# A new written-out order for one core's local-global attention with gated projection, and a new order of its first loads

## The chip, the cores and the metric

One core of one Trainium2 chip runs the whole program. The metric is device time of one execution in microseconds. Each time comes from executions on the chip; the profile is one further execution, recorded by the hardware profiler.

## What is computed

Eight batches of eight heads, 512 local and 32 global tokens, head size 64. A local token attends to the 32 global tokens and to the local ones at most 32 positions away; a global token attends to all. The heads' outputs, side by side, are a 544 x 512 matrix x per batch. It goes through a causal depthwise convolution of five taps and a sigmoid (the gate), a value product, and an output product:

```python
s_g = scale * np.matmul(q_g, k_all.transpose(0, 1, 3, 2))
out_g = np.matmul(sm(s_g), v_all)
s_ll = np.where(mask, scale * np.matmul(q_l, k_l.transpose(0, 1, 3, 2)), -1e9)
a_l = sm(np.concatenate([s_lg, s_ll], axis=-1))
out_l = np.matmul(a_l, np.concatenate([v_g, v_l], axis=2))
...
for k in range(K):
    gate_pre += conv_w[k][None, None, :] * xp[:, k:k + S, :]
gate = 1.0 / (1.0 + np.exp(-gate_pre))
return (gate * (x @ w_val) @ w_out)
```

## The kernel before

**Units and batches.** The work is cut into 32 units (one batch and two heads each, four units to a batch) and, per batch, a global part. Each is a chain of named tasks. For unit u: `s` scores (TensorE, two PSUM banks), `mx` scaled and masked scores with their maximum (VectorE, two halves of four steps), `exp` (ScalarE, two halves of four), `t` transposes of the probabilities (TensorE, two halves), `tc` their copy out of PSUM, `av` weighted values (TensorE, two banks), `eps` and `norm` the division (VectorE), `xt` the second transposes (TensorE), `xc` their copy, `halo` the four columns of the tokens before, `xh`/`xl` the high and low parts of x for the split product, `tap` and `conv` the convolution (VectorE; for units 0 and 1 on TensorE as `pc`, with diagonal matrices `dg` made by GpSimd), `sig` the tanh. The global part of batch b has `gs gmax gexp gt gtc gav geps gnorm gx gxc`. Per batch, `g1.b.e.t` are the value products (three matmuls each, high and low parts), `gv gh gl` gate the result and split it, `g2.b.r.e` the output products, `ob.b.r` copies 128 rows out of PSUM and `st.b.r` stores them. All global rows of all batches go through one more such group, `g`, at the end. `w0` to `w7` are the eight weight slices, which arrive in 64 bits; eight VectorE steps each (`s0` to `s7`) and a copy `high` split them. `z` tasks are products of zeros, in which nothing is computed.

**Order.** Nothing is scheduled at run time. `ORDER` is one list of all tasks; each engine executes its own tasks in the order of that list, and waits only for what a task depends on. `name:ENGINE` says which engine does a task that several could do, `name@57` in which PSUM banks it lives (eight banks). `Plan.add` gives each task its engine and what it depends on, `Plan.order` walks the list.

**Buffers.** Rings limit how far ahead a task may run: two buffers `ob` (shared with the weight conversion), four each for q and k (one tile, 624 KB), v (975 KB), the probabilities and xc, ten for gate, xh and xl. A copy `ob` waits until the store of the copy two before it has landed.

**Loads.** The loads named in `FIRST` are issued on SyncE's queue ahead of all tasks, in that order (`q` is a unit's q and k, `v` its values, `w` a weight slice of 512 KB, `m` the mask and convolution weights, 148 KB). Each later load (`iq`, `iv`, `wi`) is a task on SyncE, held back to its place in the list by a dependence on the TensorE instruction emitted last before it:

```python
def transfer(out, in_):
    ins = nc.sync.dma_start(out, in_).ins
    if last_pe:
        tc.add_manual_dep(ins, last_pe[0].name, after, reason="a load's place in the line")
```

Stores are issued by ScalarE in its own order (`st`), whichever engine made the copy.

Of the kernel before, what the change touches and what calls it, by code (L numbers as in the profile page):

```python
# [57 lines left out]
xh1:ACT iq6 iq7 w3.s0:ACT av2@4 eps2:DVE norm2 w3.s1 w3.s2 w4.s0:ACT w3.s3 w3.s4 xl0:ACT w4.s1 t3.1@7 pc0.2 pc0.3
pc0.4 pco0:ACT xn1 xt2@1 xc2:ACT w3.s5 pc1.0@2 w4.s2 w3.s6 w4.s3 w3.s7 tc3.1:ACT av3@4 gav0.0@7 xl1:ACT eps3:ACT w4.s4
s4@60 norm3 w4.s5 gt0.1@3 xt3@5 w3.high:ACT xh2:ACT w5.s0:ACT w5.s1 w4.high:ACT w4.s6 mx4.0 w5.s2 gtc0.1 mx4.1 xn2  # L60
w4.s7 exp4.0 w5.s3 xc3:ACT tap3:ACT pc1.1 pc1.2 gav0.1 geps0:ACT s5@34 iv4 gnorm0 w2.s0:ACT xl2:ACT w2.s1 tap2:ACT
mx5.0 mx5.1 w5.high:POOL gx0@6 gxc0:ACT halo3:ACT exp4.1 xh3:POOL pc1.3 pc1.4 pco1:ACT t4.0@3 xn3 xl3:ACT exp5.0 iv5
gs1@60 iv7 w2.s2 w2.s3 w2.high:ACT iv6 halo2:DVE s6@24 t4.1@5 tc4.1:ACT tc4.0:ACT w5.s4 w5.s5 gmax1.0 gexp1.0 conv3.0
w2.s4 conv2.0 mx6.0 exp5.1 exp6.0 gmax1.1 gexp1.1 w2.s5 mx6.1 w2.s6 exp6.1 w5.s6 g1.0.0.0@6 g1.0.0.1 g1.0.0.2 fix0
g1.0.0.3 g1.0.1.0@0 g1.0.1.1 w2.s7 gt1.0@2 t5.0@7 tc5.0:ACT av4@4 eps4:ACT t6.0@1 g1.0.1.2 w5.s7 norm4 t5.1@7
tc6.0:ACT gtc1.0 fix1 conv3.1 sig0 gv.0.0 xt4@1 xc4:ACT xh4:POOL s7@54 mx7.0 tc5.1:ACT av5@2 tap4:ACT wi6 iq8 mx7.1
sig1 eps5:ACT exp7.0 gav1.0@7 gt1.1@5 gtc1.1 conv3.2 norm5 g1.0.1.3 gv.0.1 wi7 t6.1@4 gh.0.0:ACT tc6.1:ACT conv3.3 iq9
iq10 iq11 exp7.1 gh.0.1:ACT gav1.1 geps1:DVE av6@5 eps6:ACT xt5@2 conv2.1 xn4 g1.0.2.0@0 g1.0.2.1 w6.s0:ACT xc5:ACT
xh5:ACT sig3 gnorm1 gx1@3 gxc1:ACT norm6 xt6@4 xn5 xl5:ACT halo4:ACT w6.s1 conv2.2 iv8 w6.s2 conv2.3 sig2 w6.s3 w6.s4
w7.s0:ACT xc6:ACT halo6:ACT gl.0.1 xh6:ACT tap6:ACT w7.s1 iv9 w6.s5 gl.0.0 w7.s2 w6.high:POOL g1.0.2.2 g1.0.2.3 s8@75  # L70
t7.1@6 tc7.1:ACT t7.0@3 tc7.0:ACT mx8.0 exp8.0 g1.0.3.0@2 g1.0.3.1 xn6 xl6:ACT xl4:ACT g1.0.3.2 mx8.1 exp8.1 w6.s6
g1.0.3.3 gv.0.2 t8.0@3 gv.0.3 tc8.0:ACT av7@6 s9@05 w7.s3 gs2@13 gh.0.3:ACT gh.0.2:ACT eps7:DVE norm7 xt7@6 mx9.0
# [5 lines left out]
g2.0.2.3 g2.0.3.0@0 g2.0.3.1 gt2.0@5 g2.0.3.2 s11@31 tap8:ACT xh8:ACT mx11.0 iq15 gtc2.0 gav2.0@2 gt2.1@5 ob.0.2:ACT
gtc2.1 st.0.1 t10.0@4 tc10.0:ACT t10.1@7 tc10.1:ACT av9@5 eps9:ACT mx11.1 exp11.0 norm9 gav2.1 geps2:ACT gnorm2 av10@3
eps10:ACT conv5.3 t11.0@7 exp11.1 tc11.0:ACT xt9@1 gx2@2 gxc2:DVE xc9:ACT tap9:ACT g2.0.3.3 ob.0.3:ACT s12@52 sig6  # L80
halo8:DVE iv13 norm10 xh9:ACT gs3@63 t11.1@1 tc11.1:ACT conv8.0 mx12.0 exp12.0 halo9:ACT xt10@5 xc10:ACT halo10:ACT
xh10:ACT g1.1.0.0@0 mx12.1 iv12 xl9 gmax3.0 gmax3.1 sig7 s13@21 gexp3.0 conv8.1 mx13.0 conv9.0 conv9.1 sig4 gexp3.1
# [5 lines left out]
gav3.0@4 gt3.1@2 gtc3.1 xl11 t13.1@7 xt12@0 tc13.1:ACT gl.1.1 gv.1.3 av13@1 eps13:DVE xc12:ACT tap12:ACT gav3.1 gl.1.2
geps3:DVE gnorm3 s15@73 gh.1.3:ACT gl.1.3 gx3@0 gxc3:ACT exp14.0 mx15.0 exp15.0 mx15.1 halo12:ACT xh12:ACT iv17 iq18
iq19 exp15.1 mx14.1 conv12.0 norm13 conv12.1 conv12.2 conv11.2 conv12.3 conv11.3 g2.1.0.0@4 g2.1.0.1 g2.1.0.2 g2.1.0.3  # L90
t14.0@7 g2.1.1.0@3 xl10 ob.1.0:ACT tc14.0:ACT g2.1.1.1 g2.1.1.2 s16@42 t15.1@5 xt13@0 exp14.1 t14.1@1 t15.0@6 xc13:ACT
tc14.1:ACT g2.1.1.3 g2.1.2.0@7 tc15.0:ACT av14@0 tc15.1:ACT av15@5 mx16.0 mx16.1 tap13:ACT exp16.1 t16.1@4 xh13:DVE
exp16.0 eps14:DVE norm14 xt14@2 st.1.0 tc16.1:ACT xc14:ACT halo14:ACT iv16 g2.1.2.1 tap14:ACT eps15:DVE xh14:ACT
ob.1.1:DVE st.1.1 norm15 xl13 s17@30 mx17.0 mx17.1 iv18 gs4@41 gmax4.0 exp17.0 halo13:ACT conv13.0 t16.0@6 gexp4.0
xt15@3 xc15:ACT tap15:ACT g2.1.2.2 g2.1.2.3 ob.1.2:ACT st.1.2 xh15:ACT exp17.1 t17.0@0 tc17.0:ACT gt4.0@4 iv19 gtc4.0
sig12 tc16.0:ACT conv13.1 gmax4.1 gexp4.1 halo15:DVE conv15.0 conv13.2 conv13.3 conv15.1 xl15 xl12 conv14.0 conv14.1
iq20 conv14.2 xl14 conv14.3 sig14 conv15.2 conv15.3 sig13 iq21 g2.1.3.0@3 g2.1.3.1 g2.1.3.2 g2.1.3.3 g1.2.0.0@1
ob.1.3:ACT st.1.3 g1.2.0.1 g1.2.0.2 g1.2.0.3 gv.2.0 gh.2.0:DVE g1.2.1.0@5 g1.2.1.1 g1.2.1.2 g1.2.1.3 av16@6 gav4.0@2
gv.2.1 s18@04 s19@31 mx18.0 t17.1@5 g1.2.2.0@0 eps16:ACT exp18.0 norm16 xt16@6 g1.2.2.1 mx18.1 gh.2.1:DVE gl.2.1
tc17.1:ACT exp18.1 sig15 gt4.1@4 gtc4.1 mx19.0 g1.2.2.2 t18.0@7 exp19.0 gav4.1 geps4:ACT av17@4 tc18.0:ACT mx19.1  # L100
xc16:DVE xh16:ACT gnorm4 gx4@3 gxc4:ACT halo16:ACT tap16:DVE t18.1@1 g1.2.2.3 g1.2.3.0@3 tc18.1:ACT gl.2.0 iq22
g1.2.3.1 conv16.0 conv16.1 conv16.2 iq23 conv16.3 sig11 g1.2.3.2 g1.2.3.3 iv22 exp19.1 s20@67 sig16 eps17:DVE av18@1
gv.2.2 gv.2.3 norm17 gh.2.2:DVE gh.2.3:DVE xt17@0 xc17:ACT gl.2.2 halo17:ACT mx20.0 exp20.0 gl.2.3 xl16 eps18:DVE
norm18 mx20.1 tap17:DVE conv17.0 conv17.1 conv17.2 xh17:ACT xl17 g2.2.0.0@3 g2.2.0.1 g2.2.0.2 t19.1@6 tc19.1:ACT iv21
iv20 g2.2.0.3 g2.2.1.0@4 g2.2.1.1 xt18@0 xc18:ACT conv17.3 tap18:ACT g2.2.1.2 g2.2.1.3 ob.2.1:ACT sig17 g2.2.2.0@2
exp20.1 g2.2.2.1 gs5@46 gmax5.0 gmax5.1 st.2.1 s21@01 xh18:DVE t19.0@4 xl18 tc19.0:ACT t20.0@5 tc20.0:ACT t20.1@6
mx21.0 g2.2.2.2 mx21.1 g2.2.2.3 ob.2.2:DVE tc20.1:ACT av19@4 eps19:DVE av20@0 norm19 eps20:DVE gexp5.0 gt5.0@6
# [870 lines left out]
```

## Time and profile before

| | us |
|---|---|
| median of 3 runs | 363.06 (360.9 to 363.09) |
| the profiled execution | 362.68 |
| its span, first to last instruction | 360.9 |
| TensorE busy | 349.5 |
| VectorE busy | 307.2 |
| ScalarE busy | 233.6 |
| GpSimd busy | 10.4 |

The time of an execution is its span and 1.8 us around it. Matmuls overlap in the pipeline and their ends are modelled, so a busy TensorE may still be losing time; the profile's view by stretches gives busy time and the granted clock for any part of the span. A wait is put down to what came last. SPq and ACTq are the queues on which SyncE and ScalarE issue DMAs.

### The profile page before, as it was taken

What the parts mean: (1) busy time and instruction counts of PE and PEld (TensorE: products, weight loads), DVE (VectorE), ACT (ScalarE), POOL (GpSimd) and SP (SyncE); (2) the same over time, 40 slices, a digit from 0 to 9 for tenths busy, and PEclk for the clock granted to TensorE, in tenths of its full rate; (3) what the DMA queues carried; (4) which work ended last, traced back from release to release, by engine and by line L of the source; (5) the groups of instructions that cost most, each with busy time, mean ns of one, the idle gap of its engine ahead of it and who ended that gap; (6) DMA issues with size and microseconds to landing.
All of it is one profiled execution on the core that took longest, in us unless ns stands there. A gap on an engine that the chain in (4) does not pass through costs nothing.

```text
span 360.9 us, 14693 instructions
## 1 busy us (share of the span) xinstructions
PE 349.5 (97%) x6339; PEld 282.1 (78%) x6339; DVE 307.2 (85%) x1027; ACT 233.6 (65%) x587; POOL 10.4 (3%) x23
## 2 busy tenths in 40 slices
...
GB/s 298 396 399 293 177 272 256 370 127 344 121 348 281 113 177 319 248 14 308 189 181 307 139 322 146 107 143 181 289 96 3 4 39 81 0 58 35 83 59 58
DMA packets 17104, 66.59 MB, mean 185 GB/s; under 512 B 1808, under 2 KB 3984, under 8 KB 17040
## 3 DMA queue, kind: packets, MB, share of 16 engines
...
## 4 chain that ended last, share of the span: by engine, by line
PE 82%; DMA 7%; DVE 6%; ACT 2%; issue 1%; SPq 1%; DVEq 0%; ACTq 0%
PE psum L646 26%; PE psum L674 20%; PE psum L522 8%; PE psum L533 8%; PE psum L497 7%; DMA out_dram<-ob 4%; PE psum L552 4%; DMA v<-in_vw_dram 3%; PE psum L462 2%; PE psum L618 2%; PE psum L442 2%; PE psum L423 1%; DVE gate L234 1%; DVE pm L234 1%; PE psum L444 1%
## 5 line engine op out<-in xcount | busy, mean ns | idle before, releaser
L234 DVE SCALAR_TENSOR_TENSOR gate<-xc,cw,gate 128x512 f32<-128x512 f32 x120 | 87.6, 749 | 4.8 <-ACT xc L329 2.6
L516 ACT ACTIVATE pm<-pm,mx 128x128 f32<-128x128 f32 x256 | 80.8, 393 | 11.8 <-DVE mx L234 11.2
L234 DVE CUSTOM_DVE_ANT_0 pm<-psum,small 128x128 f32<-128x128 f32 x256 | 57.3, 287 | 4.7 <-PE psum L497 4.7
L646 PE MATMUL psum<-xh,wvh 128*128 128x512 f32 x128 | 53.0, 414 | 0.0
L674 PE MATMUL psum<-woh,gh 128*128 128x512 f32 x128 | 52.3, 408 | 0.0
L646 PE MATMUL psum<-xl,wvh 128*128 128x512 f32 x128 | 50.9, 397 | 0.0
L646 PE MATMUL psum<-xh,wvl 128*128 128x512 f32 x128 | 50.5, 394 | 0.0
L674 PE MATMUL psum<-woh,gl 128*128 128x512 f32 x128 | 50.2, 392 | 0.0
L674 PE MATMUL psum<-wol,gh 128*128 128x512 f32 x128 | 50.0, 390 | 0.0
L522 PE MATMUL psum<-ident,pm 128*128 128x128 f32 x256 | 39.2, 281 | 3.5 <-ACT ob L322 3.1
L522 PEld LDWEIGHTS psum<-ident,pm 128*128 128x128 f32 x256 | 29.5, 142 | 12.0 <-ACT ob L322 4.0
L322 ACT ACTIVATE ob<-psum 128x512 f32<-128x512 f32 x26 | 15.4, 592 | 36.3 <-PE psum L674 23.2
L497 PE MATMUL psum<-qk 64*32 64x128 f32 x2048 | 36.8, 276 | 0.9 <-issue 0.9
L329 ACT COPY pts<-psum 128x512 f32<-128x512 f32 x54 | 30.5, 583 | 9.8 <-PE psum L522 9.4
L497 PEld LDWEIGHTS psum<-qk 64*32 64x32 f32 x2048 | 29.4, 107 | 8.7 <-issue 5.2
L533 PE MATMUL psum<-v,pts 128*32 128x65 f32 x2048 | 35.0, 221 | 1.2 <-DMA v<-in_vw_dram 0.7
L533 PEld LDWEIGHTS psum<-v,pts 128*32 128x32 f32 x2048 | 30.5, 109 | 7.1 <-issue 4.6
L234 DVE SCALAR_TENSOR_TENSOR gv<-gate,psum 128x512 f32<-128x512 f32 x32 | 21.5, 683 | 10.8 <-PE psum L646 10.7
L630 ACT ACTIVATE gate<-gate 128x512 f32<-128x512 f32 x32 | 20.0, 629 | 13.5 <-DVE gate L234 12.9
L646 PEld LDWEIGHTS psum<-xh,wvl 128*128 128x128 f32 x128 | 24.3, 190 | 5.6
L646 PEld LDWEIGHTS psum<-xh,wvh 128*128 128x128 f32 x128 | 24.5, 192 | 4.9 <-DVE gm L234 0.4
L674 PEld LDWEIGHTS psum<-woh,gl 128*128 128x128 f32 x128 | 24.0, 188 | 5.3
...
## 6 DMA issues: line engine op xcount, KB each, us to landing
...
wraw<-in_w_val_dram SPq DMA_DIRECT2D x4, 512.0 KB, 12.5
...
```

Of the source, the lines that this page charges most:

```text
L234: ins = made(*args, **kwargs)
L322: A.activation(out=out, in_=in_, func=AF.Copy, scale=by)
L329: A.copy(out, in_)
L442: on_pe(T.transpose(pt[:96, 1 + a, :], pg[:, 96 * a:96 * a + 96], ident))
L497: on_pe(T.matmul((sx, sy)[h][32 * j:32 * j + 32, i, :], qkt[rows, 32 * m:32 * m + 32], qkt[rows, k0:k0 + P], start=True, stop=True))
L516: A.activation(out=pm[:, h, i, :], in_=pm[:, h, i, :], func=AF.Exp, bias=mx[:, c:c + 1], scale=-1.0)
L522: on_pe(T.transpose(pt[:, i, :], pm[:, h, i, :], ident))
L533: on_pe(T.matmul(ax[32 * j:32 * j + 32, h, E1 * i:E1 * i + E1], pts[:, h, i, 32 * j:32 * j + 32], vt[:, block_win(4 * i + j), h, :], start ...
L552: on_pe(T.matmul(xt[:, P * i:P * i + P], xs[:, i].rearrange("p h d -> p (h d)"), ident, start=(i == 0 or u not in XP), stop=(u not in XP), ...
L630: A.activation(out=g, in_=g, func=AF.Tanh, scale=0.5)
L646: on_pe(T.matmul(box["pv", e], w[:, e, t * P:t * P + P], x, start=(t == 0 and q == 0), stop=(t == NDT - 1 and q == 2)))
L674: on_pe(T.matmul(box["po", r], g[:, e, rs], w[:, e, :], start=(e == 0 and q == 0), stop=(e == NDT - 1 and q == 2)))
```

## The change

`ORDER` is replaced by another list of the same 1,480 tasks besides the `z` tasks: another sequence on every engine, other PSUM banks, other engines for some steps (about equally many go from ScalarE to VectorE and back; a few more go to GpSimd), and other places for the later loads and stores. The zero products are six in three tasks (`z1.0`, `z4.1`, `z1.2`) instead of three in two. In `FIRST`, q and k of unit 2 and the values of unit 0 go ahead of the first weight slice, and the values of units 2 and 3 go ahead of the third and fourth. No task's code changes. The two lists have over a hundred lines each; the beginning, two later places and the end are shown.

```diff
 ORDER = """
-s0@50 s1@12 cw dg0 mx0.0 exp0.0 t0.0@5 mx0.1 mx1.0 w0.s0:ACT exp1.0 z2.0@3 t1.0@7 tc0.0:ACT s2@34 wi4 w0.s1 w0.s2
-exp0.1 t0.1@6 w0.s3 w0.s4 w0.high:ACT mx2.0 mx2.1 tc0.1:ACT z1.1@0 av0@0 dg1 eps0:DVE gs0@35 mx1.1 exp2.1 norm0 exp2.0
-xt0@2 gmax0.0 exp1.1 t1.1@0 gexp0.0 iq4 s3@41 tc1.0:ACT xc0:ACT gmax0.1 gexp0.1 tc1.1:ACT w1.s0:DVE w1.s1 w1.s2 wi5
...
-w7.s4 w7.s5 av8@1 gl.0.3 t9.0@7 tc9.0:ACT g2.0.0.2 w7.s6 gexp2.0 iq12 tap7:ACT iv10 w7.s7 s10@53 mx10.0 exp10.0 iv11
...
-av11@6 mx13.1 iq16 iq17 xl8 eps11:ACT norm11 iv14 exp13.0 tap10:ACT conv10.0 conv9.2 conv10.1 t12.0@5 tc12.0:ACT
...
-g2.4.0.0@2 s28@16 gv.4.3 mx28.0 tc26.1:ACT av26@4 gav6.1 iv30 tc27.0:ACT av27@0 eps26:ACT norm26 geps6:DVE xt26@4
-exp28.0 gnorm6 gx6@7 mx28.1 g2.4.0.1 g2.4.0.2 gh.4.3:ACT iv31 gl.4.3 g2.4.0.3 g2.4.1.0@6 g2.4.1.1 g2.4.1.2 eps27:DVE
...
-xl26 iv29 ob.4.0:ACT st.4.0 halo26:ACT conv24.2 conv24.3 tap26:ACT xh25:ACT xl25 g2.4.1.3 g2.4.2.0@5 g2.4.2.1 g2.4.2.2
-ob.4.1:ACT conv26.0 conv26.1 conv26.2 sig24 xc27:ACT xh27:ACT conv25.2 conv25.3 conv26.3 tap27:ACT st.4.1 halo27:DVE
-conv27.0 conv27.1 g2.4.2.3 ob.4.2:ACT st.4.2 sig26 iv28 conv27.2 conv27.3 g2.4.3.0@2 t28.1@1 tc28.1:ACT g2.4.3.1
-g2.4.3.2 g2.4.3.3 ob.4.3:ACT st.4.3 g1.5.0.0@3 g1.5.0.1 gs7@64 gmax7.0 s29@01 mx29.0 gmax7.1 exp29.0 mx29.1 exp29.1
-t28.0@2 tc28.0:DVE g1.5.0.2 g1.5.0.3 gv.5.0 g1.5.1.0@6 gexp7.0 g1.5.1.1 g1.5.1.2 g1.5.1.3 gv.5.1 t29.1@0 tc29.1:DVE
...
+cw s0@31 dg0 dg1 s1@62 mx0.0 exp0.0 mx0.1 mx1.0 exp0.1 s2@10 wi4 mx2.0 mx2.1 exp1.0 z1.0@4 t1.0@7 tc1.0:DVE mx1.1
+exp2.0 exp2.1 t0.0@5 tc0.0:DVE exp1.1 w0.s0:DVE w0.s1 t0.1@4 tc0.1:ACT z4.1@3 av0@6 eps0:ACT gs0@40 t2.1@3 tc2.1:ACT
+w0.s2 w0.s3 norm0 xt0@2 iq4 iq5 gmax0.0 t1.1@6 w0.s4 w0.s5 xc0:ACT t2.0@3 halo0 s3@74 wi5 tc1.1:ACT z1.2@5 av1@5 w0.s6
+gmax0.1 iq6 xh0:ACT mx3.0 mx3.1 w1.s0:ACT gexp0.1 pc0.0@0 iq7 w1.s1 xn0 tc2.0:ACT eps1:DVE norm1 w0.s7 w1.s2 w1.s3
+xt1@3 exp3.0 w1.high:POOL exp3.1 t3.0@4 xc1:DVE xl0:ACT pc0.1 w1.s4 gexp0.0 w0.high:ACT w1.s5 w1.s6 w1.s7 tc3.0:ACT
...
+w6.s7 iq12 g2.0.0.0@2 tap4:ACT iv9 iq13 g2.0.0.1 w7.s6 gl.0.2 xn7 xl7:ACT s10@67 w7.s7 gh.0.3:ACT gl.0.3 gexp2.0
...
+mx13.0 xl9 g1.1.0.1 mx13.1 exp13.1 g1.1.0.2 g1.1.0.3 norm11 xt11@5 xc11:ACT halo10:ACT conv8.0 conv8.1 conv8.2 t12.0@2
...
+g2.4.0.2 iv29 tap22:ACT conv22.0 g2.4.0.3 conv23.1 ob.4.0:ACT st.4.0 g2.4.1.0@3 exp28.1 g2.4.1.1 g2.4.1.2 g2.4.1.3
+g2.4.2.0@1 g2.4.2.1 g2.4.2.2 g2.4.2.3 ob.4.1:DVE st.4.1 conv23.2 halo25:ACT conv22.1 eps27:ACT exp28.0 iq31 ob.4.2:ACT
+conv22.2 xt26@2 iv31 g2.4.3.0@0 g2.4.3.1 g2.4.3.2 g2.4.3.3 g1.5.0.0@3 conv22.3 g1.5.0.1 norm27 xt27@5 ob.4.3:DVE
+conv23.3 xc26:ACT iv28 xl23 g1.5.0.2 g1.5.0.3 conv24.3 t28.0@7 gv.5.0 g1.5.1.0@1 xc27:DVE tc28.0:DVE sig21 s29@03
+gs7@46 mx29.0 exp29.0 gmax7.0 t28.1@2 tap26:DVE iv30 mx29.1 tc28.1:DVE g1.5.1.1 t29.0@4 g1.5.1.2 g1.5.1.3 exp29.1
...
+xh25:ACT halo26:DVE xl25 t30.1@5 tc30.1:ACT g2.5.0.0@6 g2.5.0.1 g2.5.0.2 gav7.1 conv25.0 gh.5.3:DVE st.4.3 tc30.0:ACT
+av30@3 tc31.0:DVE av31@1 xt29@0 tap27:DVE gl.5.3 g2.5.0.3 st.4.2 conv25.1 conv25.2 g2.5.1.0@5 g2.5.1.1 g2.5.1.2
...
+conv30.3 gh.7.0:ACT gl.7.0 ob.6.1:DVE ob.5.2:ACT st.5.2 sig30 sig29 gv.7.1 gv.7.2 g1.7.3.3 g2.7.0.0@4 gh.7.1:DVE
+gl.7.1 gh.7.2:DVE gl.7.2 st.6.1 ob.6.3:ACT gv.7.3 gh.7.3:DVE gl.7.3 ob.5.0:DVE g2.7.0.1 gxl1 g2.7.0.2 st.6.3 g2.7.0.3
+g2.7.1.0@0 st.5.0 ob.7.0:ACT st.7.0 gconv3 sigg3 g2.7.1.1 g2.7.1.2 g2.7.1.3 g2.7.2.0@3 gxh3:DVE gxl3 gtap1:DVE gconv1
+ob.7.1:ACT st.7.1 gtap2:DVE g2.7.2.1 g2.7.2.2 g2.7.2.3 g2.7.3.0@0 g2.7.3.1 g2.7.3.2 gxh0:DVE gxl0 g2.7.3.3 g1.g.0.0@2
+ob.7.3:ACT gconv2 g1.g.0.1 gxl2 g1.g.0.2 g1.g.0.3 sigg2 gtap0:DVE gconv0 sigg0 gv.g.0 st.7.3 gh.g.0:DVE gl.g.0
...
 """
...
-FIRST = "q0 m0 q1 w0 q2 v0 q3 w1 v1 w2 v2 w3 v3"
+FIRST = "q0 m0 q1 q2 v0 w0 q3 w1 v1 v2 w2 v3 w3"
```

## Rows read from the trace of the kernel before

**Rows 1.** The page, its first part: busy time of each engine, its share of the span, and its instructions.

```profile
PE 349.5 (97%) x6339; PEld 282.1 (78%) x6339; DVE 307.2 (85%) x1027; ACT 233.6 (65%) x587; POOL 10.4 (3%) x23
```

**Rows 2.** The chain of waits in order of time, pieces in which TensorE runs one kind of step without a gap: start, us, engine, line, instructions. L646 are the value products, L674 the output products, L497 a unit's scores (64 instructions), L533 its weighted values (64), L522 its transposes (8), L423 a batch's global scores (32), L462 one half of the global values (40), L618 one tap of a convolution on TensorE (2).

```profile
20.39 0.86 PE psum L618 x2
...
42.11 1.08 PE psum L423 x32
...
57.81 0.71 PE psum L462 x40
...
272.26 0.87 PE psum L522 x8
273.13 1.95 PE psum L533 x128
...
277.60 1.96 PE psum L497 x128
...
301.49 10.99 PE psum L646 x48
312.92 10.91 PE psum L674 x48
...
345.69 5.65 PE psum L646 x48
351.34 5.46 PE psum L674 x24
```

**Rows 3.** TensorE's timeline: the second transposes (of the normalized values xs) of units 2, 16, 27, 28 and of the last one (30). Start us, us, engine, line, operation, tiles, shape, count.

```profile
30.34 0.60 PE L552 MATMUL psum<-ident,xs 128*128 128x128 f32 x4
...
154.15 0.63 PE L552 MATMUL psum<-ident,xs 128*128 128x128 f32 x4
...
252.20 0.60 PE L552 MATMUL psum<-ident,xs 128*128 128x128 f32 x4
...
275.60 0.60 PE L552 MATMUL psum<-ident,xs 128*128 128x128 f32 x4
...
312.32 0.60 PE L552 MATMUL psum<-ident,xs 128*128 128x128 f32 x4
```

**Rows 4.** The table by stretches of the span: busy time of each engine with its instructions in brackets (TensorE, its weight loads, VectorE, ScalarE, GpSimd), then the granted clock as a share of 2.4 GHz, the mean busy share of the DMA engines, and GB/s.

```profile
0.00:27.00 27.00, 22.97 (x533) 14.64 (x533) 19.96 (x101) 19.69 (x51) 8.00 (x19) 1.00 0.96 364
27.00:120.00 93.00, 92.84 (x2109) 73.34 (x2105) 90.43 (x322) 83.14 (x211) 2.40 (x4) 1.00 0.66 252
120.00:252.00 132.00, 131.92 (x2711) 109.22 (x2700) 121.80 (x425) 90.43 (x236) 0.00 (x0) 1.00 0.54 195
...
262.80:265.90 3.10, 0.04 (x4) 0.00 (x1) 3.06 (x17) 0.60 (x1) 0.00 (x0) 0.99 0.19 68
265.90:269.20 3.30, 3.30 (x10) 2.82 (x11) 1.39 (x9) 2.94 (x9) 0.00 (x0) 0.50 0.22 82
269.20:357.00 87.80, 87.59 (x864) 73.67 (x863) 59.70 (x142) 30.54 (x71) 0.00 (x0) 1.00 0.11 40
```

**Rows 5.** The timeline of the first 30 us, all engines, in order of time; in brackets how long the engine stood before the row, and for what. The rows are the scores of unit 1 (weight loads), the first two maxima of unit 0, its first group of exponentials, the scores of unit 2, the issue of v3 on SyncE's queue, three groups of exponentials in one, and the weighted values of unit 0.

```profile
6.72 0.89 PEld L497 LDWEIGHTS psum<-qk 64*32 64x32 f32 x64 [0.15 <-DMA qk<-in_qk_dram]
...
6.96 0.29 DVE L234 CUSTOM_DVE_ANT_0 pm<-psum,small 128x128 f32<-128x128 f32 x1 [0.46 <-PE psum L497]
...
7.18 0.28 DVE L234 CUSTOM_DVE_ANT_0 pm<-psum,small 128x128 f32<-128x128 f32 x1
...
7.30 1.28 ACT L516 ACTIVATE pm<-pm,mx 128x128 f32<-128x128 f32 x4 [5.09 <-DVE mx L234]
...
10.63 1.16 PE L497 MATMUL psum<-qk 64*32 64x128 f32 x64
...
12.19 3.51 SPq L347 DMA_DIRECT2D v<-in_vw_dram  x1
...
13.02 3.62 ACT L516 ACTIVATE pm<-pm,mx 128x128 f32<-128x128 f32 x12
...
13.29 1.11 PE L533 MATMUL psum<-v,pts 128*32 128x65 f32 x64 [0.69 <-DMA v<-in_vw_dram]
```

**Rows 6.** The place near 84 and the place near 265: a piece of the chain of waits (a store that was waited for); two v loads on SyncE's queue (start, time of the two issues); ScalarE's timeline with the issue of st.4.1 and the copy ob.4.3; TensorE's with t28.0; and the time from issue to landing of the DMAs that read the copies ob, from the view of that tile.

```profile
83.85 6.45 DMA out_dram<-ob
...
252.83 3.78 SPq L347 DMA_DIRECT2D v<-in_vw_dram  x2
...
256.55 0.34 ACTq L855 DMA_DIRECT2D out_dram<-ob  x1
...
265.25 0.60 ACT L322 ACTIVATE ob<-psum 128x512 f32<-128x512 f32 x1 [3.79 <-DMA out_dram<-ob]
...
265.90 1.11 PE L522 MATMUL psum<-ident,pm 128*128 128x128 f32 x4 [3.06 <-ACT ob L322]
...
DMA to landing us min/median/max: 2.0/2.6/8.3
```

**Rows 7.** The timelines of VectorE and TensorE at two hand-overs: gl.0.3 (VectorE) and the first output product that reads it, the second step of unit 11's normalization (xs) and its transposes.

```profile
76.88 0.69 DVE L234 TENSOR_TENSOR gl<-gv,gh 128x512 fp32r<-128x512 f32 x1
...
78.92 0.39 PE L674 MATMUL psum<-woh,gh 128*128 128x512 f32 x1
...
106.01 0.69 DVE L234 TENSOR_TENSOR xs<-psum,mx 128x512 f32<-128x512 f32 x1
...
107.56 0.60 PE L552 MATMUL psum<-ident,xs 128*128 128x128 f32 x4
```

More of the change, by code (lines that the diff above doesn't have):

```diff
@@ L58 @@
[L58 to L72, printed above, removed]
@@ L78 @@
[L78 to L82, printed above, removed]
@@ L88 @@
[L88 to L107, printed above, removed]
@@ L123 @@
-g1.4.1.0@0 g1.4.1.1 g1.4.1.2 g1.4.1.3 halo23:ACT conv23.0 eps24:DVE norm24 conv23.1 conv23.2 exp26.0 t26.0@2
-tc26.0:DVE gv.4.0 gv.4.1 gh.4.1:DVE conv23.3 exp27.1 xt24@1 xc24:ACT xh24:DVE gav6.0@3 sig23 av25@4 eps25:DVE norm25
-gh.4.0:ACT tap24:ACT xl24 iq30 iq31 gl.4.0 gl.4.1 exp26.1 xl23 gt6.1@1 g1.4.2.0@6 g1.4.2.1 g1.4.2.2 g1.4.2.3 xt25@7
-t27.1@0 tc27.1:DVE g1.4.3.0@5 gtc6.1 gv.4.2 gh.4.2:DVE xc25:ACT gl.4.2 g1.4.3.1 g1.4.3.2 t26.1@4 t27.0@0 g1.4.3.3
-g2.4.0.0@2 s28@16 gv.4.3 mx28.0 tc26.1:ACT av26@4 gav6.1 iv30 tc27.0:ACT av27@0 eps26:ACT norm26 geps6:DVE xt26@4
@@ new lines @@
+exp2.0 exp2.1 t0.0@5 tc0.0:DVE exp1.1 w0.s0:DVE w0.s1 t0.1@4 tc0.1:ACT z4.1@3 av0@6 eps0:ACT gs0@40 t2.1@3 tc2.1:ACT
+w0.s2 w0.s3 norm0 xt0@2 iq4 iq5 gmax0.0 t1.1@6 w0.s4 w0.s5 xc0:ACT t2.0@3 halo0 s3@74 wi5 tc1.1:ACT z1.2@5 av1@5 w0.s6
+gmax0.1 iq6 xh0:ACT mx3.0 mx3.1 w1.s0:ACT gexp0.1 pc0.0@0 iq7 w1.s1 xn0 tc2.0:ACT eps1:DVE norm1 w0.s7 w1.s2 w1.s3
+xt1@3 exp3.0 w1.high:POOL exp3.1 t3.0@4 xc1:DVE xl0:ACT pc0.1 w1.s4 gexp0.0 w0.high:ACT w1.s5 w1.s6 w1.s7 tc3.0:ACT
+av2@5 eps2:DVE norm2 gt0.0@1 xh1:ACT xn1 halo1 w4.s0:DVE xl1:ACT w4.s1 w4.s2 w4.s3 gtc0.0 w4.s4 pc0.2 pc0.3 pc0.4
```

134 lines of the change are left out of this document (85 added, 49 removed).

## Prediction, before the changed kernel was run

> **What bounds the kernel now.** The page's table of engines comes first: TensorE is busy for 97% of the span, VectorE 85%, ScalarE 65% [rows 1]. That share is an average, and TensorE's ends are modelled, so the second view is the chain of waits, read for runs of one kind with nothing between them. They give what each step costs when TensorE streams [rows 2]: 48 value products in 10.99 us, 48 output products in 10.91, the last (global) group 5.65 and 5.46, a unit's scores 0.98 (1.96 for two), its weighted values 0.975, its eight transposes of probabilities 0.87, a global score step 1.08, a global value step 0.71, one tap of a convolution on TensorE 0.86. A batch's products are 21.9 us, eight batches 175.2, the global group 11.1; 32 units of scores, values and transposes are 31.4 + 31.2 + 27.8; their second transposes, at half of 0.87, 13.9; 16 global value steps 11.4, 8 global scores 8.6, 80 global transposes at 0.109 are 8.7, ten taps 8.6, small ones (10 products of 512 columns and 8 single transposes, at 0.229 and 0.109) 2.7. Together 331 us. The change keeps all of them, so only about 30 us of the 360.9 can move.
>
> Where these 30 us lie is read from TensorE's own timeline: start of a second transpose, less the work ahead of it in the order. I call this the lag. It is 12.7 us at unit 2 (30.34, with 17.6 us of work ahead), 17.8 at unit 16 (154.15, 136.4), 20.65 at unit 27 (252.20, 231.55), 25.7 at unit 28 (275.60, 249.9) and 26.0 at the last (312.32, 286.3) [rows 3]; from the end of the last product, 356.8, to the end of the span another 4.1 pass [rows 2]. So 12.7 go in the first 30 us, 8 drip away over the next 220 (changes of kind, stalls of tenths), 5 go in one place near 265, and the last 90 us lose nothing. The table by stretches says who else is near its limit: VectorE is busy 90.4 of 93 us between 27 and 120 and 121.8 of 132 up to 252, but 59.7 of 87.8 at the end [rows 4]. For two thirds of the kernel VectorE is a second bound right behind TensorE.
>
> **Part 1: the first loads.** The 13 loads are the same; unit 2's q and k and v0 pass the first weights. Before, s1 starts at 6.72, as its data lands, and s2 at 10.63 [rows 5]. A 624 KB load at the 364 GB/s of the stretch 0 to 27 takes 1.7 us [rows 4], so q2 now lands near 8.4. But s2 also writes a bank that the eighth maximum of unit 0 sets free; the maxima start at 6.96 and follow one another 0.22 us apart [rows 5], so s2 goes at about 8.8, 1.8 us earlier. This is lost again at the next step. The new order puts six groups of exponentials on ScalarE ahead of tc0.1, which av0 needs: 7.30 plus six times 1.2 (12 in 3.62) is 14.5, plus 0.6 for the copy 15.1 [rows 5]. Before, av0 waited for v0 until 13.29. So v0's earlier landing buys nothing, and av0 is 1.8 us later. The conversion of w0 starts near 13.7 instead of 8.5; nothing of TensorE asks for w0 before g1.0.0.0, 25 us later, and the VectorE time freed is taken by maxima and by two copies. Following both orders on with these durations, the set up to av2 (scores 0 to 3, seven transposes, av0 to av2, gs0, xt0, xt1, two taps, xn0, gt0.0: 14.35 us, the same set in both) ends at 27.1 before and near 26.7 after. SyncE's later queue does not move: its ring is full until 15.7 either way (12.19 + 3.51, rows 5), and 8.6 MB come first in both. I take -0.3 us, bounds -1.0 and +1.0. Six filler products instead of three run while TensorE has nothing else: 0, at most 0.7 if all three sit on the path.
>
> **Part 2: VectorE in the first 120 us.** The counts per step stay; who does them changes (net +6.6 us for VectorE, most of it late, by counting both lists at row durations). What matters is the work of VectorE ahead of a step that TensorE waits for, against TensorE's own ahead of the consumer. For unit 11's normalization it was 103.1 against 91.1, and is 101.7 against 87.9: 1.8 us less margin. The margin before was 0.9 (its norm done at 106.7, its transposes at 107.56). For gl.0.3 there is 2.9 less, with 1.4 before (done 77.6, used 78.92) [rows 7]. So TensorE would wait some 1.5 us at the first and 0.9 at the second. These do not add: the second is the same queue, already late. What remains is the excess over the lag that before reaches anyway (17.8 at unit 16 against some 18.2), 0.4 to 0.9. I take +0.6; bounds 0 and +1.8.
>
> **Part 3: the stall near 265.** Here ScalarE stands before ob.4.3 for the buffer of ob.4.1, whose store went out at 256.55 and landed 8.3 us later; the median is 2.6 [rows 6]. Ahead of it lie four v loads of 975 KB, the last two issued at 252.83. The copy starts at 265.25, frees bank 2, and t28.0 starts at 265.90. TensorE stood 3.06 us, and in the stretch behind it the granted clock is 0.50, that is 1.2 GHz, for 3.3 us, in which four transposes and six products ran that cost 1.8 at 2.4 GHz [rows 2, 4, 6]. The lag says 5.0 for the whole place; less 0.3 for ordinary drip it is 4.7. In the new order the four v loads of this batch stand apart (iv29 before g2.4.0.3, iv31 after g2.4.2.3, iv28 after ob.4.3, iv30 after gs7), so at most one load and iq31 lie near st.4.1; t28.0 no longer uses the bank of g2.4.3; and ob.4.3 is on VectorE. I take -4.7, bounds -5.0 and 0.
>
> The row shows a store that landed only once the loads ahead of it were through. The Trainium skill, page "DMA: Bandwidth & Descriptors", section "Queues, rings and completion order", says that each DMA engine takes turns between the queues, packet by packet. By that rule the store on ScalarE's queue would go on at about half its rate beside the loads, which adds an estimated 0.7 us (256 KB at 364 GB/s) to 2.6; the loads would not be the cause, and setting them apart would give nothing. The trace's 8.3 us speaks against it, and so does the 6.45 of a second store, at 83.85, with loads about it [rows 6]; but these are two stores.
>
> **Part 4: the late half.** VectorE has 80 us of steps left from g1.5.0.0 on, where it had 61, against 92 of TensorE. Three places are close: xl23 behind ob.4.3 (0.45 us before g1.5.0.3), gl.7.3 (0.4 before g2.7.0.3), gxl2 behind three global convolutions (0.7 before g1.g.0.2), each worked out by following the lists from the last step at which VectorE waits for TensorE. ob.4.3 on VectorE is a new wait: behind it stand conv23.3, xl23, conv24.3 and gv.5.0, and g1.5.0.3 waits for xl23. With a landing of 2.6 us it costs nothing; with one of 6 it costs 2 to 3. The stores st.4.2 and st.4.3 now wait 24 to 32 us, and ob.5.0 and ob.5.2 hold two of eight banks for 40; no PE step asks for these banks before the global group. I take +0.7, bounds 0 and +3. The last 4.1 us are the same two copies and stores.
>
> **The sum.** -0.3 + 0.6 - 4.7 + 0.7 = -3.7 us. The profiled execution took 362.68 (span 360.9 and 1.8 around it), so 359.0. The median of the runs is 363.06, so this is 1.1% below it; 1%, 3.6 us, is about what a measurement of this kernel can tell from no change.
>
> **Rivals.** (a) *The store stall comes back*, because one load is enough, or because it was not the loads. The price is the whole of part 3: a store held 8 us makes VectorE stand 3 us at ob.4.3, TensorE at g1.5.0.3, and the half clock follows. 362.68 - 0.3 + 0.6 + 0.7 = 363.7. For it: iv31 and iq31 still leave right behind st.4.1, and both slow stores. Against it: they leave behind it, not ahead of it, and half of the stores land within 2.6 [rows 6]. By the page's rule above, this is the case that comes. (b) *VectorE becomes the bound between 27 and 120.* Its busy share there is 97% [rows 4], and the orders' margins shrink by up to 2.9. Each microsecond that VectorE idles more than before in that stretch (it idles 2.6) is then lost by TensorE too, one for one. From 4 us of extra idling the change is slower than before; at 8, a loss of 0.3 us at each of some 27 hand-overs, it is 367.0. Against it: the new order also gives ScalarE less, so fewer waits for it. (c) *All close places hold.* -1.0 at the start, nothing in parts 2 and 4, -4.7: 357.0. For it: each margin in part 4 is positive.
>
> **Chances and range.** Forecast 0.50, of which a third lies above the 1% mark; (a) 0.22; (b) 0.14, most of it above 366.7; (c) 0.14. Faster by over 1%: 0.33 + 0.14 = 0.47; within 1%: 0.17 + 0.22 + 0.03 = 0.42; slower: 0.11. The range runs from just below (c), 356.0, to past (a), 365.0.
>
> **What would show it.** In the profile after: s2 near 8.8 and av0 near 15; a lag at unit 2 or 3 of 12.5 to 13.5; a lag of 18 to 18.5 at unit 16; no gap of TensorE over 1 us between 250 and 270, no half clock there, and st.4.1 landing in under 5 us; and the last 90 us dense, with the lag at the last transpose near 22. I am wrong if av0 starts much later than 15, if VectorE idles over 5 us between 27 and 120, or if ob.4.3 on VectorE shows a wait for a store of over 2 us.

## The result and the profile after

The changed kernel is slower. Its median is 365.2 us (362.6 to 367.3, 20 runs); the kernel before, on the same chip, takes 362.4 (360.5 to 364.1, 20 runs). The ratio is 1.0071, 95% interval 1.0052 to 1.0091, so 2.8 us are lost where 3.7 were to be won. The profiled execution took 366.13 (span 364.3), 3.45 more than that of before.

The table by stretches comes first, with the columns of [rows 4]:

```profile
0.00:27.00 27.00, 21.35 (x477) 13.78 (x477) 19.54 (x99) 17.86 (x47) 7.88 (x19) 1.00 0.95 355
27.00:120.00 93.00, 90.43 (x1976) 71.25 (x1971) 85.92 (x307) 73.58 (x191) 5.57 (x10) 0.98 0.65 248
120.00:252.00 132.00, 130.32 (x2658) 108.28 (x2654) 115.17 (x406) 88.67 (x230) 0.61 (x1) 1.00 0.52 185
250.00:270.00 20.00, 20.00 (x314) 16.69 (x313) 17.34 (x45) 8.64 (x25) 0.00 (x0) 1.00 0.49 164
```

Near 265 the expected gain is there: TensorE is busy for all of 250 to 270, at full clock, where it stood 3.06 us and then ran at half clock [rows 4, 6]. The loss is earlier. Between 27 and 120 TensorE idles 2.6 us instead of 0.2, between 120 and 252 it idles 1.7 instead of 0.1. TensorE's timeline says where. The bracket is how long the engine stood before the row, and for what; "issue" is a pause for which the profile has no releaser.

```profile
9.56 1.15 PE L497 MATMUL psum<-qk 64*32 64x128 f32 x64 [0.49 <-DVE mx L234]
...
14.64 1.26 PE L533 MATMUL psum<-v,pts 128*32 128x65 f32 x64 [1.27 <-DVE pts L234]
...
20.69 0.86 PE L497 MATMUL psum<-qk 64*32 64x128 f32 x39 [1.05 <-issue]
...
55.87 0.40 PE L646 MATMUL psum<-xh,wvh 128*128 128x512 f32 x1 [0.34 <-issue]
...
61.61 0.36 PE L533 MATMUL psum<-v,pts 128*32 128x65 f32 x10 [2.19 <-issue]
...
61.82 1.31 PE L462 MATMUL psum<-v,pgt 96*32 96x65 f32 x37
...
165.06 1.19 PE L533 MATMUL psum<-v,pts 128*32 128x65 f32 x68
167.34 1.10 PE L533 MATMUL psum<-v,pts 128*32 128x65 f32 x60 [1.09 <-issue]
...
229.23 1.16 PE L497 MATMUL psum<-qk 64*32 64x128 f32 x64 [0.59 <-ACT ob L322]
```

Two of the four unnamed pauses break off a unit's weighted values in the middle: av6, with 11 of its 64 instructions left (10 in one row), and av18, with 60 left (the 68 instructions ahead of the pause are the 64 of av17 and four of av18; the expectations below call this the pause in av17). The instructions left over read the same two tiles as those already done. Behind the pause in av6 the clock falls: 37 steps of gav1.0 take 1.31 us where 40 took 0.71 [rows 2], and between 62 and 64 us the granted clock is 0.50, that is 1.2 GHz:

```profile
62.00:64.00 2.00, 2.00 (x44) 1.80 (x37) 1.19 (x2) 0.72 (x3) 0.00 (x0) 0.50 0.04 8
```

Put as the lag of the prediction, the difference to before at the same work ahead is +1.5 us at unit 3, +6.4 behind unit 6, +6.2 at unit 16, +7.3 at unit 17, +8.0 at unit 23, +3.4 at unit 28 and +3.45 at the last. So: +1.5 at the start, +4.9 between 42 and 67 us, +1.1 at av18, +0.7 near 225, -4.7 near 265, nothing behind it.

**What the pauses have in common.** Number TensorE's instructions in the order of the list: each matmul is a load of weights and a multiplication, and an f32 product that is no transpose runs as two such pairs (the trace has 2048 of L533 for 1024 in the list). The 55 waits of the sequencer that the trace has between them (`EVENT_SEMAPHORE` and `DRAIN`) count as well. Up to the pause in av6 the view of line L533 counts

```profile
L533 PE MATMUL psum<-v,pts x437: 217/220/245, 14.6 to 59.2; 128*32 128x65 f32 x146
```

and ahead of the 438th stand 1243 pairs of all lines and 11 waits, so it is instruction 2498, which is 9 x 256 + 194. The four pauses above lie at 706, 2241, 2498 and 7105: the remainder by 256 is 193 or 194 each time. It is so for the two unnamed pauses of the kernel before (705 and 962), and for all 33 of the twelve profiled executions shown here. Where it is 193, that load still ran and its multiplication, number 194, was held; so the first instruction held is number 194 of a block each time. The profile's list of DMA queues has a line that I had read past. After the colon: packets, MB, share of the 16 engines.

```profile
q8 instruction: 49, 0.80, 0.9%
```

These are 49 packets of 16 KB for the 49.8 blocks of 256 instructions that TensorE has. The same view, cut to short windows of the changed kernel, gives the time of each. From 55.9 to 59.0 there is only data (first row); the packet starts in the tenth from 59.2 on (second):

```profile
q1 hardware_dynamic: 298, 1.20, 98.6%
...
q8 instruction: 1, 0.02, 61.1%
```

TensorE goes on at 61.61, 2.4 us later. For the pauses that end at 55.87 and 167.34 the packets start at 53.5 and 165.0, in the kernel before for 19.14 at 16.8: 2.3 to 2.4 us each time, and 2.2 to 2.7 over all 33. In stretches with few loads most packets start 0.1 to 1.1 us after TensorE has passed the border before (passed 253.8, packet in the half microsecond from 254.0); ahead of the pause in av6 it was 3.4 (59.26 after 55.87). So the theory: at each border the next block is asked for; the packet stands behind the loads already on the DMA engines; and if TensorE needs less time for 256 instructions than that delay and 2.4 us, it stands. A unit's weighted values are 128 instructions in 0.975 us, so 256 of that kind pass in 2 us; 256 of the products take 29 (128 times 10.99/48) [rows 2].

The Trainium skill, page "Runtime: NRT & Kernel Launch", section "Instruction fetch mechanics", says that instructions come in blocks of 256 by DMA while the block before runs, and that the cost of crossing a border is "mostly hidden". The first half agrees with these rows. The second holds for most of the some 590 crossings of the twelve profiled executions, and not for 33 of them, which cost 0.25 to 3.55 us each.

### The profile page after: what moved, and what is told of

It reads as the page before. It is cut to its first block, busy times and chain, and to the rows that moved or that the text cites. A ratio compares the mean times of both kernels' runs of the same rounds, so it can differ in the third digit from the quotient of the medians.

```text
span 364.3 us, 14720 instructions
## 1 busy us (share of the span) xinstructions
PE 350.3 (96%) x6342; PEld 283.8 (78%) x6342; DVE 312.8 (86%) x1038; ACT 223.6 (61%) x570; POOL 14.1 (4%) x29
## 4 chain that ended last, share of the span: by engine, by line
PE 91%; DMA 4%; DVE 2%; issue 2%; ACT 1%; SPq 0%; ACTq 0%
PE psum L646 26%; PE psum L674 24%; PE psum L497 9%; PE psum L533 9%; PE psum L522 8%; PE psum L552 4%; PE psum L462 3%; PE psum L618 2%; PE psum L423 2%; DMA out_dram<-ob 2%; PE psum L442 2%; DMA qk<-in_qk_dram 2%; DVE pm L234 1%; PE psum L444 1%; ACT ob L322 0%
## 5 line engine op out<-in xcount | busy, mean ns | idle before, releaser
L234 DVE SCALAR_TENSOR_TENSOR gate<-xc,cw,gate 128x512 f32<-128x512 f32 x120 | 88.7, 749 | 2.0
L646 PE MATMUL psum<-xh,wvh 128*128 128x512 f32 x128 | 53.1, 415 | 0.3 <-issue 0.3
L674 PE MATMUL psum<-woh,gh 128*128 128x512 f32 x128 | 52.2, 408 | 0.0
L646 PE MATMUL psum<-xl,wvh 128*128 128x512 f32 x128 | 50.4, 394 | 0.0
L674 PE MATMUL psum<-woh,gl 128*128 128x512 f32 x128 | 50.2, 392 | 0.0
L646 PE MATMUL psum<-xh,wvl 128*128 128x512 f32 x128 | 50.2, 392 | 0.0
L674 PE MATMUL psum<-wol,gh 128*128 128x512 f32 x128 | 50.0, 391 | 0.0
L497 PE MATMUL psum<-qk 64*32 64x128 f32 x2048 | 37.3, 278 | 3.0 <-issue 1.0
L533 PE MATMUL psum<-v,pts 128*32 128x65 f32 x2048 | 35.0, 221 | 4.6 <-issue 3.3
L533 PEld LDWEIGHTS psum<-v,pts 128*32 128x32 f32 x2048 | 30.7, 110 | 10.3 <-issue 7.3
L497 PEld LDWEIGHTS psum<-qk 64*32 64x32 f32 x2048 | 29.5, 107 | 10.6 <-issue 4.4
L522 PE MATMUL psum<-ident,pm 128*128 128x128 f32 x256 | 37.3, 276 | 0.0
L522 PEld LDWEIGHTS psum<-ident,pm 128*128 128x128 f32 x256 | 29.6, 141 | 6.9 <-issue 1.7
L234 DVE SCALAR_TENSOR_TENSOR gv<-gate,psum 128x512 f32<-128x512 f32 x32 | 21.7, 683 | 8.2 <-PE psum L646 5.8
L646 PEld LDWEIGHTS psum<-xh,wvl 128*128 128x128 f32 x128 | 24.0, 188 | 5.5
L674 PEld LDWEIGHTS psum<-woh,gl 128*128 128x128 f32 x128 | 24.0, 188 | 5.3
L646 PEld LDWEIGHTS psum<-xh,wvh 128*128 128x128 f32 x128 | 24.2, 189 | 4.7 <-ACT gate L329 0.3
L674 PEld LDWEIGHTS psum<-woh,gh 128*128 128x128 f32 x128 | 24.2, 189 | 4.5
```

The source lines that it names most:

```text
L234: ins = made(*args, **kwargs)
L497: on_pe(T.matmul((sx, sy)[h][32 * j:32 * j + 32, i, :], qkt[rows, 32 * m:32 * m + 32], qkt[rows, k0:k0 + P], start=True, stop=True))
L522: on_pe(T.transpose(pt[:, i, :], pm[:, h, i, :], ident))
L533: on_pe(T.matmul(ax[32 * j:32 * j + 32, h, E1 * i:E1 * i + E1], pts[:, h, i, 32 * j:32 * j + 32], vt[:, block_win(4 * i + j), h, :], start ...
L646: on_pe(T.matmul(box["pv", e], w[:, e, t * P:t * P + P], x, start=(t == 0 and q == 0), stop=(t == NDT - 1 and q == 2)))
L674: on_pe(T.matmul(box["po", r], g[:, e, rs], w[:, e, :], start=(e == 0 and q == 0), stop=(e == NDT - 1 and q == 2)))
```

## The experiments

Their ratios are to the kernel before, run beside each of them; they are estimates of their own and need not equal the quotient of the two medians.

**Three loads out of the way.**

```diff
-wi6 iq8 wi7 w2.s5
+w2.s5
-av6@1 gav1.0@7
+av6@1 wi6 iq8 wi7 gav1.0@7
```

> The changed kernel, with the loads wi6, iq8 and wi7 moved in the list from ahead of w2.s5 to behind av6, nothing else. Theory (the fetch of TensorE's own instructions): TensorE stands still for 2.19 us inside av6 because the block of instructions it needs next is a packet on the DMA engines, asked for when the block before it was begun (near 55.9) and held up until 59.0 by these three loads. With the loads behind av6 the packet starts within 1 us of 55.9, the pause inside av6 falls from 2.19 us to under 0.5 us, the half-clock stretch behind it goes too, and the kernel is 2 to 3.5 us faster than the changed kernel (365.2): 361.7 to 363.2. Rival one (the pause is av6's own, a wait on data or on the loads' issue): the pause stays and the time is 365 +- 0.7. Rival two (the loads are needed early, w6.s0, iq8): the pause goes but ScalarE's w6.s0 or s8 waits over 2 us, time 364 to 366.

Measured: 364.4 us, ratio 1.0043 (1.0012 to 1.0075). The pause goes as the theory has it, and the wait and the time of rival two come true. In the DMA view from 55.9 to 56.9 the instruction packet is the only one, and starts at 56.4:

```profile
q8 instruction: 1, 0.02, 6.0%
```

TensorE's timeline has no pause in av6, but these:

```profile
66.47 1.38 PE L497 MATMUL psum<-qk 64*32 64x128 f32 x64 [2.84 <-DMA qk<-in_qk_dram]
...
167.87 1.10 PE L533 MATMUL psum<-v,pts 128*32 128x65 f32 x60 [1.65 <-issue]
```

At units 5 and 6 the lag is 3.5 to 4.1 us below that of the changed kernel; then s8, waiting for iq8, and slower steps behind it give it all back by 73 us. The place was right; this cure was not.

**Each half of the change alone.** The changed list with the old first loads, and the old list with the new ones:

```diff
-FIRST = "q0 m0 q1 q2 v0 w0 q3 w1 v1 v2 w2 v3 w3"
+FIRST = "q0 m0 q1 w0 q2 v0 q3 w1 v1 w2 v2 w3 v3"
```

> The changed kernel's task list with the first loads in the order of the kernel before (w0 ahead of q2, w1 ahead of v1): one half of the change taken back. Theory (the new first loads cost the start): q1 lands near 6.7 instead of 7.9, the 2.1 us that the second transposes of the first units have lost by 11 us of TensorE's work fall to under 1 us; 363.5 to 364.5 against 365.2 of the changed kernel. Rival (the list needs the new loads): s2 waits for q2 until near 11, av0 comes near 16, the time is 365.2 to 367.

> The kernel before with the first loads in the order of the changed kernel, its task list as it was: the other half alone. Theory (the new first loads cost the start): q1 lands 1.2 us later and w0 2 to 3 us later, which VectorE's steps w0.s0 and on wait for; the time is 363 to 365 against 362.4. Rival (the loads have room): 362.4 +- 0.7. Second rival (values earlier help): 361 to 361.7.

Measured: 367.7, ratio 1.0154 (1.0090 to 1.0219), and 367.0, ratio 1.0127 (1.0070 to 1.0183). For the first the rival holds, at a time above its range: s2 waits for q2 (and the pause in av6 is 2.99 us), as TensorE's timeline shows. In the second the wait is larger than forecast: ScalarE's first step on w0 waits 5.26 us for it, and a unit's transposes on TensorE behind it 4.18 (second and third fence).

```profile
11.00 1.15 PE L497 MATMUL psum<-qk 64*32 64x128 f32 x64 [1.96 <-DMA qk<-in_qk_dram]
...
63.46 0.36 PE L533 MATMUL psum<-v,pts 128*32 128x65 f32 x10 [2.99 <-issue]
```

```profile
13.35 0.66 ACT L289 ACTIVATE wa<-wraw 128x512 f32<-128x512 f32 x1 [5.26 <-DMA wraw<-in_w_val_dram]
```

```profile
14.35 1.35 PE L522 MATMUL psum<-ident,pm 128*128 128x128 f32 x4 [4.18 <-ACT pm L516]
```

Each list needs its own loads; neither half alone is a gain.

**The stall near 265 without the rest of the change.** One load of the kernel before, moved:

```diff
-sig26 iv28 conv27.2
+sig26 conv27.2
-ob.4.3:ACT st.4.3 g1.5.0.0@3
+ob.4.3:ACT st.4.3 iv28 g1.5.0.0@3
```

> The kernel before with the one load iv28 moved in the list from behind st.4.2 to behind st.4.3, nothing else. The prediction's part 3 says that the store st.4.1 (issued 256.55, landed 8.3 us later) is held up by the v loads issued at 252.83 to 256.6, and that ob.4.3's wait for it costs 4.7 us with the half clock behind it. Theory: st.4.1 lands in under 5 us, ob.4.3 waits under 0.5 us, no half clock near 266; 357.5 to 358.5 against 362.4. Rival (the other load, iv29, alone holds the store up): the store still lands in over 7 us, 361 to 362.4. Rival (the instruction fetch or av28 takes it back): the wait goes but TensorE pauses elsewhere between 262 and 290, 359 to 361.

Measured: 359.5 us, ratio 0.9920 (0.9886 to 0.9955): faster than both kernels. The trace is as the theory has it: the stores between 245 and 272 land within 4.9 us, st.4.1 itself in 3.4, TensorE has no pause there, the clock stays up. So the one load was enough. In the row of [rows 6] it is the second of the two issues, at 256.28, just ahead of the store (256.55); the row's 252.83 is the first.

The view of the tile ob in that stretch, the table by stretches, and TensorE's one long pause:

```profile
DMA to landing us min/median/max: 2.4/3.4/4.9
```

```profile
262.00:270.00 8.00, 8.00 (x127) 6.20 (x126) 7.79 (x29) 4.71 (x12) 0.00 (x0) 1.00 0.47 167
```

```profile
21.01 0.66 PE L497 MATMUL psum<-qk 64*32 64x128 f32 x29 [1.77 <-issue]
```

From unit 27 to unit 28 the lag falls by 4.6 against before, the 4.7 of part 3. But the median falls by 2.9 (by the ratio) to 3.5 only. The runs of before suggest why: beside this kernel 8 of 19 ran at a granted clock of 0.997 or more over the whole span and took 361.5 on the mean, 11 at 0.991 to 0.995 and took 363.9; of this kernel's ten, nine ran at 0.997 or more and took 359.4. So the full price of the stall, with its half clock, seems to be in about half of the executions of before. Both profiled ones (clock 0.995 and 0.993) were of that half; none of the other half was profiled, so this is argued, not shown.

**More instructions of no use.** To the filler z1.1 of the kernel before, near 13 us, 64 tiny matmuls are added (extra; 128 instructions, half a block), then 128 of them (256 instructions, a whole block):

```diff
         for _ in range(n):
             on_pe(T.matmul(psum[:, b, :], z[:, :P], z, start=True, stop=True))
+        for _ in range(extra):
+            on_pe(T.matmul(psum[:, b, :16], z[:, :P], z[:, :16], start=True, stop=True))
```

> The kernel before with 64 extra, tiny matmuls (16 columns, into a free bank) in the filler z1.1 near 12 us, where TensorE has little to do; nothing else is added or moved. They are 128 instructions of TensorE (each a weight load and a matmul), half of the 256 after which its pauses lie, and cost 1 to 2 us by themselves. Theory (fetch): every later block border falls 128 instructions earlier in the list, onto places that were not chosen with it, so that pauses appear at new places, wherever 256 short instructions follow each other while loads fill the DMA engines; worked out from the trace of before by the rule (next block usable 2.35 us after its packet starts, packet starts when the loads ahead of it are done) the pauses sum to some 10 us or more: 368 to 380, and every pause without a named releaser lies at the same remainder of the instruction number. Rival (the pauses are tied to the tasks, not to the count): the pause in s3 stays where it was, and the time is that of the kernel before plus 1 to 2 us, 363.5 to 365.5.

> As the run before it, with 128 extra tiny matmuls: 256 instructions, one whole block. Theory (fetch): behind the filler the borders fall on the same instructions of the list as in the kernel before, so the pauses from 19 us on are those of the kernel before; what is left is the cost of the extra matmuls themselves, 2 to 4 us at most: 363 to 367, less than with half as many. Rival (what costs is the extra matmuls): twice the extra cost of the run with 64.

Measured: 386.8 us (1.0622, 1.0592 to 1.0652) with 64, 385.4 us (1.0637, 1.0596 to 1.0678) with 128. The cost of the matmuls themselves was missed by far: 11 us for 64 and 22 for 128, at the start, most of it at half clock. So the numbers of both expectations are off, and the times alone tell little; the traces tell the theories apart. With half a block TensorE's timeline (the first row is of the tiny matmuls) and the table by stretches have

```profile
13.38 11.14 PE L747 MATMUL psum<-zr 128*128 128x16 f32 x64
...
67.76 0.25 PE L533 MATMUL psum<-v,pts 128*32 128x65 f32 x2 [1.10 <-issue]
...
120.89 0.42 PE L533 MATMUL psum<-v,pts 128*32 128x65 f32 x12 [2.37 <-issue]
...
254.71 0.41 PE L497 MATMUL psum<-qk 64*32 64x128 f32 x6 [3.55 <-issue]
```

```profile
53.00:279.00 226.00, 211.41 (x4464) 172.90 (x4462) 196.34 (x682) 157.57 (x404) 1.23 (x2) 0.98 0.54 199
```

The three pauses are of ten unnamed pauses, 12.4 us in all, none of them where before has one, and each at the remainder 193 or 194 of the longer list. TensorE idles 14.6 us in 226, the clock falls behind two of the pauses, and the lag over before grows from 11.3 us at 53 to 31.5 at 279 (at the end it is 27.4, since the stall near 265 is missing here). Loads held up the packet at two of the ten, those of 120.89 and 254.71: it started 4.1 and 4.4 us after the border before. At the other eight it started 0.2 to 1.2 us after it; there TensorE was through the 256 instructions in 2.0 to 3.2 us, too soon even without a load in the way. Ahead of the pause at 67.76 the view of the DMA queues from 64 to 67 has the instruction packet alone:

```profile
q8 instruction: 1, 0.02, 2.7%
```

With a whole block there is no unnamed pause at all, where the expectation had those of before. The same stretch, and the second transposes of [rows 3] but for unit 28's:

```profile
53.00:279.00 226.00, 225.63 (x4804) 184.09 (x4804) 213.54 (x745) 174.58 (x449) 2.41 (x4) 1.00 0.58 215
```

```profile
52.48 0.60 PE L552 MATMUL psum<-ident,xs 128*128 128x128 f32 x4
...
176.43 0.63 PE L552 MATMUL psum<-ident,xs 128*128 128x128 f32 x4
...
274.53 0.60 PE L552 MATMUL psum<-ident,xs 128*128 128x128 f32 x4
...
333.97 0.60 PE L552 MATMUL psum<-ident,xs 128*128 128x128 f32 x4
```

They come 22.1, 22.3, 22.3 and 21.7 us behind those of before: once the filler is through, nothing more is lost in 280 us. Tasks, loads and engines are the same in both; besides 64 more tiny matmuls at the start, only the place of the borders differs. The pauses hang on the count.

**Five loads out of the way.** The changed kernel, with iq8 up instead of down:

```diff
-s7@72 gtc1.0
+s7@72 iq8 gtc1.0
-wi6 iq8 wi7 w2.s5
+w2.s5
-av6@1 gav1.0@7
+av6@1 wi6 wi7 gav1.0@7
-conv15.0 iq22 t18.0@6 gtc4.1 t18.1@5 iq23 g1.2.2.2
+conv15.0 t18.0@6 gtc4.1 t18.1@5 g1.2.2.2
-av17@2 eps17:DVE
+av17@2 iq22 iq23 eps17:DVE
```

> The changed kernel with five loads moved out of the way of the two long instruction fetches: iq8 up behind s7, wi6 and wi7 down behind av6, iq22 and iq23 down behind av17. Theory (fetch): the pauses in av6 (2.19 us) and in av17 (1.09 us, 1.65 in the run with three loads moved) fall to under 0.4 us each, and with iq8 earlier s8 doesn't wait for it as it did (2.84 us): 360.5 to 362 against 365.2. Rival (a later reader gives it back, as s8 did): w6's first step on ScalarE or s22 waits over 1.5 us and the time is 363 to 365.

Measured: 362.2 us, ratio 0.9984 (0.9958 to 1.0011): a little above what the theory named, 3.2 us less than the changed kernel by the two ratios. Of the two pauses 0.28 us is left, at av18; at unit 6 the lag is 4.1 below that of the changed kernel, at the end 5.6. w6's first step waits 0.67 us, s22 not at all. VectorE, whose work is the same, idles 3.4 us between 27 and 120, not 7.1. TensorE's timeline and the table by stretches:

```profile
162.67 1.10 PE L533 MATMUL psum<-v,pts 128*32 128x65 f32 x60 [0.28 <-issue]
```

```profile
27.00:120.00 93.00, 92.42 (x2171) 73.31 (x2164) 89.62 (x327) 76.27 (x201) 5.67 (x10) 1.00 0.67 251
```

**Second looks.** Before, changed, and changed with five loads moved, each profiled once more:

> The kernel before, unchanged: a second profiled execution. The first had q1 landing early (s1 at 6.72 without a wait), where every other kernel here with whatever order waits for q1 until 7.85 to 8.33, and it had the store st.4.1 landing after 8.3 us. Theory (the profiled execution was not a typical one at the start): s1 waits for q1 until about 8, the start up to 25 us is 1 to 2 us longer. If the store's late landing is in every execution, ob.4.3 waits 3 to 4 us again; if it is in about half of them (the times of the kernel before spread from 360.3 to 365.7), it may be missing, and then the time is 360 to 361.5. Rival (the profiled execution was typical): s1 at 6.7 again.

> The changed kernel, unchanged: a second profiled execution. Theory (fetch behind the three loads): the pause inside av6 is there again within 1 us of 2.19, with the clock fallen behind it or not, since loads and list are the same; the pause in av17 likewise. Rival (an accident of the one execution): no pause above 0.5 us in av6.

> The changed kernel with the five loads moved, unchanged: a second profiled execution, since its median (362.2) lies 1.6 us above the one profiled (360.6). Theory (the start varies): the same list loses its 1 to 2 us ahead of 30 us. Rival (a store or a fetch that is late in some executions): a wait of 1 to 3 us behind 200 us, on an output copy or without a named releaser.

Measured: 364.8, 364.8 and 363.1 us, one execution each. In the kernel before s1 waits for q1 until 8.08, the start is 1.3 to 1.9 us longer, as the theory had it, and the stall near 265 is there again. The changed kernel has the same pauses in av6 and av18. In the third the start is no later than in its first look (0.75 us earlier); a store near 220 is, as the rival had it, and it costs 1.2 us. The rest of the 2.5 us between the two looks is 1.1 between units 3 and 8, in part waits for VectorE (0.56, near 65) and ScalarE (0.45, near 69), and 1.0 outside the span (363.06 less 360.3, against 1.8). TensorE's timelines, in that order:

```profile
8.08 1.16 PE L497 MATMUL psum<-qk 64*32 64x128 f32 x64 [1.19 <-DMA qk<-in_qk_dram]
...
31.69 0.60 PE L552 MATMUL psum<-ident,xs 128*128 128x128 f32 x4
...
268.01 0.66 PE L522 MATMUL psum<-ident,pm 128*128 128x128 f32 x4 [2.90 <-ACT ob L322]
```

```profile
61.16 0.36 PE L533 MATMUL psum<-v,pts 128*32 128x65 f32 x10 [2.46 <-issue]
...
166.79 1.10 PE L533 MATMUL psum<-v,pts 128*32 128x65 f32 x60 [1.38 <-issue]
```

```profile
225.31 1.16 PE L497 MATMUL psum<-qk 64*32 64x128 f32 x64 [0.97 <-ACT ob L322]
```

## Why the prediction was wrong

**Part 1, -0.3 at the start.** Followed step by step it held: av0 at 14.64 for 15.1; s2 at 9.56 for 8.8. The lag at unit 3 was 14.7 where 12.5 to 13.5 was named. The fault is in what it was compared with: in the profiled execution of before q1 landed at 6.7, in all the others here, whatever their order, at 7.4 to 8.3. The second look at before has a lag of 14.8 at the same work, so against a usual start the term is -0.1 (-0.7 by the second look at the changed kernel, 14.1). The run with iv28 moved, which has the first loads of before, starts like the second look at before (lag 14.3 at unit 3 in both).

**Part 2, +0.6 while VectorE is tight.** About right. Between units 6 and 16 the difference in lag stays at 6.1 to 6.5; in the kernel with five loads moved, where nothing else hides it, it grows by 0.5, and by 1.1 in its second look. VectorE did idle over 5 us in that stretch (7.1), which I had named as the sign of rival (b); but it idled because TensorE stood, and with the loads moved it idles 3.4. An idle second engine says that the first one waited for it only where a wait for it is shown.

**Part 3, -4.7 near 265.** The mechanism and the size are right: -4.7 in the profile of the changed kernel, -4.6 with one load moved alone. The estimate by which the store goes on beside the loads, so that they are not the cause, fails: with that load issued later the store landed after 3.4 us instead of 8.3. Set against the median it was too large: alone the stall is worth 2.9 by the ratio, probably because it has its full price in only about half of the executions. A store was held up elsewhere instead (issued 221.38, landed 6.55 us later, behind v loads issued at 216.65 and 220.07): 0.7 us here, 1.2 in the last look, nothing in two other looks. That is a small piece of rival (a), at another place.

**Part 4, +0.7 in the late half.** Nothing was lost: the lag grows by 0.4 from unit 28 to the end, 0.3 before.

**The step that failed** is one ahead of the four parts: of the 30 us that can move, the prediction took the 8 that "drip away over the next 220 (changes of kind, stalls of tenths)" as fixed but for part 2, since "the change keeps all of them", the 331 us of TensorE's steps. It does keep them, but their instructions have to arrive, and when they arrive depends on the order. The new order puts av5 and av6 right behind each other while wi6, iq8 and wi7 fill the DMA engines, so 256 instructions pass in less time than the next block needs. That is +4.1 us with the half clock (1.1 more at av18) in the profile, and 3.2 us in the median, by the run that moves the loads. It stood in no term and no rival. The signs were in the trace of before: two unnamed pauses, at 19.14 and 26.11, which I had booked as stalls of the start, and the queue's line on the page. How much hangs on where the borders fall in an order, the run with half a block shows.

**What stays open.** -0.1 + 0.5 - 2.9 + 3.2 give 0.7, the measurement 2.8. The remaining 2.1 us are barely clear of noise: by the intervals of the two ratios that they rest on they could be some 1.6 more or less. Candidates are the store near 221, more of part 2, and time outside the span (up to 2.8 us with the new order, at most 1.84 in the 33 runs of before for which it is on record); no run isolates any of them. Nor was it tried to cure the pauses by spreading the short steps rather than the loads.
